# Letting GpSimd take some of the softmax scalings in a planned attention and MLP kernel

## The chip, the cores and the metric

The kernel runs on one core of a Trainium2 chip. The metric is the device time of one execution in microseconds (us); three timed runs of the kernel before gave a median of 614.84 us (614.14 to 614.98). The engines are PE (TensorE), DVE (VectorE), ACT (ScalarE), POOL (GpSimd) and SP (the queue that issues the DMAs).

## What is computed

Attention with a window of 128 keys and 4 sink keys, for 2 batches, 8 heads, 768 positions and 64 values per head; its output is taken as 1536 tokens of 512 values and goes through two MLPs with 2048 hidden values, all in float32:

```python
a = np.exp(scores - max)                      # scores outside window and sinks are -1e9
a = a / (np.sum(a, axis=-1, keepdims=True) + 1e-09)
attn = np.matmul(a, v)
h = x @ w_in;  x = (h * np.clip(h + 3.0, 0.0, 6.0) / 6.0) @ w_out       # first MLP
h = x @ w2_in; out = (h * (1.0 / (1.0 + np.exp(-1.702 * h)))) @ w2_out  # second MLP
```

## The kernel before

The attention goes over 12 tiles of 128 tokens, each in two halves of four heads, called duos (`duo`, 24 in all). A duo's steps are: the scores on PE into two PSUM banks (L756); per head, on DVE, scale, mask and row minimum (L771); per head, on ACT, the exponential with its row sum in a column of `z` (L779); one `inverse` on DVE (L787 adds 1e-9, L788 takes the reciprocal of the four sums); per head, **the scaling** `pexp <- pexp * z`, a multiplication of 128x196 numbers by one number per partition; two `turn`s on PE, eight transposes of the scaled P into PSUM (L807); copies of them to SBUF (`pts`). After two duos come the values on PE (L830, L838), and their result is split into a rounded part `xyh` (ACT) and a rest `xyl` (DVE, L857).

The MLPs multiply in three products of rounded parts and rests. A block of 512 tokens and one of 16 slices of the hidden layer make an item: the up product (L541, 12 matmuls), the activation on ACT and DVE (L553 and L558 in the first MLP), the split of its result into `gh` and `gl` (L584), and the down product (L609, 12 matmuls). Each weight slice is loaded into one of two `stage` buffers and brought into its final form once per MLP: one ACT instruction (L452) and four on DVE (L457, L465, L473, L480). A buffer is loaded again when L480 has read it. In every item the weights are split again (L430 or L432 the rounded part, L522 the rest, on DVE).

All of this is recorded as operations with a list of engines and costs in nanoseconds, and a planner (`Plan.issue`) fixes the order on each engine before the program is built. At each step it computes for every operation that is ready, and for each of its engines, when it could start (the engine free, its inputs finished, plus a fixed lag between engines) and takes the engine with the lowest score:

```python
for eng, cost in o.opts:
    x = max(t, at[eng])
    for d in o.deps:
        x = max(x, d.finish + self.lag(d.eng, eng))
    score = x + cost * (1 + early[eng])
```

`early` adds half of the cost on DVE (`PDVE` 0.5), 15 % on ACT (`PACT` 0.15) and nothing on POOL. On the chip each engine then works through its list in that order, and waits where an input is late. POOL has nothing in its list before this change but the set-up (constants, the identity, index grids).

Of the kernel before, what the change touches and what calls it, by code (L numbers as in the profile page):

```python
# [14 lines left out]
ALU = mybir.AluOpType  # L15
# [48 lines left out]
def tile_sink_window_attention_moe_moe2(  # L64
# [10 lines left out]
    nc = tc.nc  # L75
# [150 lines left out]
    with tc.tile_pool(name="msk", bufs=1) as mp:  # L226
# [15 lines left out]
            out=out, in0=grid, scalar1=x, scalar2=LOW, op0=op, op1=ALU.mult  # L242
# [185 lines left out]
    def copy(eng, out, in_):  # L428
        if eng is nc.scalar:
            eng.copy(out, in_)  # L430
        else:
            eng.tensor_copy(out, in_)  # L432
# [264 lines left out]
    def plan_attention(plan, pool, due):  # L697
# [28 lines left out]
        def duo(d, pts):  # L726

            T, half = divmod(d, 2)
            i = tok[T][1]
            kind = min(i, 2)  # L730
            front = T - 1 if i else T
            when = None
            sc = [Buf(cls="bank", kind="s") for j in range(2)]
            nbs, z = [Buf(cls="nb") for _ in range(4)], Buf(cls="z")
            pes = [Buf(cls="pexp") for _ in range(4)]

            def scores(e):

                for a in range(2):
                    hp = 2 * half + a  # L740
                    k0, q0 = hp * KW, NPAIR * KW + hp * P
                    here, before = kqt[T], kqt[front]
                    for x in range(3):
                        for c in range(2):
                            if x == 0:
                                src, at, n = before, k0, HALF
                            elif x == 1:
                                src, at, n = here, k0 + TAIL, HALF
                            elif c == 0:
                                src, at, n = before, k0 + HALF, TAIL  # L750
                            else:
                                src, at, n = here, k0, TAIL
                            for j in range(2):
                                r = slice(j * D, (j + 1) * D)
                                o = a * W + x * HALF
                                e.matmul(  # L756
                                    sc[j].tile[c * HALF : (c + 1) * HALF, o : o + n],
                                    here[r, q0 + c * HALF : q0 + (c + 1) * HALF], src[r, at : at + n],
                                    start=True, stop=True,
                                )  # L760

            plan.op(
                [("PE", 1050)], scores, when, reads=[kq_b[t] for t in sorted({front, T})], writes=sc, chain="scores",
            )
            heads = [(a, j) for a in range(2) for j in range(2)]
            for a, j in heads:
                n = 2 * a + j
                cols = slice(a * W, (a + 1) * W)
                plan.op(
                    [("DVE", 283)],  # L770
                    lambda e, j=j, n=n, cols=cols: e.tensor_tensor_reduce(  # L771
                        out=pes[n].tile[:, :W], in0=sc[j].tile[:, cols], in1=masks[kind],
                        scale=-SCALE, scalar=LOWEST, op0=ALU.add, op1=ALU.min, accum_out=nbs[n].tile,
                    ),
                    when, reads=[sc[j], mask_b[kind]], writes=[pes[n], nbs[n]],
                )
                plan.op(
                    [("ACT", 410)],
                    lambda e, n=n: e.activation(  # L779
                        pes[n].tile[:, :W], pes[n].tile[:, :W], AF.Exp,  # L780
                        bias=nbs[n].tile, scale=-1.0, accum_out=z.tile[:, n : n + 1],
                    ),
                    when, reads=[nbs[n]], writes=[pes[n]], adds=[z], chain="exp",
                )

            def inverse(e):
                e.tensor_scalar(out=z.tile, in0=z.tile, scalar1=1e-9, scalar2=None, op0=ALU.add)  # L787
                e.reciprocal(z.tile, z.tile)  # L788

            plan.op([("DVE", 280)], inverse, when, writes=[z])  # L790
            for n in range(4):

                def scale(e, n=n):
                    x, r = pes[n].tile[:, :W], z.tile[:, n : n + 1]
                    if e is nc.scalar:
                        e.mul(x, x, r)
                    else:
                        e.tensor_scalar_mul(x, x, r)

                plan.op([("DVE", 232), ("ACT", 350)], scale, when, reads=[z], writes=[pes[n]])  # L800
            for a in range(2):
                pt, pb = Buf(cls="bank", kind="t"), Buf(cls="pts")

                def turn(e, a=a, pt=pt):
                    for n in range(4):
                        j, x = divmod(n, 2)
                        e.transpose(  # L807
                            pt.tile[:, n * P : (n + 1) * P], pes[2 * a + j].tile[:, x * P : (x + 1) * P], ident
                        )

                plan.op([("PE", 440)], turn, when, reads=pes[2 * a : 2 * a + 2], writes=[pt], chain="turn")
                plan.op(
                    [("ACT", 478), ("DVE", 602)],
                    lambda e, pt=pt, pb=pb: copy(e, pb.tile, pt.tile.rearrange("p (n t) -> p n t", t=P)),
                    when, reads=[pt], writes=[pb],
                )
                pts.append(pb)
# [47 lines left out]
        for T in range(NTILE):  # L865
            pts = []
            for half in range(2):
                duo(2 * T + half, pts)
            tile_values(T, pts)

            if T + 2 < NTILE:
                load(T + 2)
# [211 lines left out]
```

## Time and profile before

| | |
|---|---|
| median of three runs | 614.84 us |
| the profiled execution, its own time | 615.07 us |
| span of the profiled execution (first to last instruction) | 613.3 us |
| busy: PE / DVE / ACT / POOL | 586.0 / 451.3 / 360.8 / 1.4 us |
| scalings of 128x196: on DVE / on ACT | 59 / 37 |

The profiled execution took 1.8 us more than its span. A busy PE is not a PE at full pace: matmuls overlap, and in a stretch where nothing is late 94 or 95 matmuls of 128x512 fit in 20 us. Idle time counts only where the engine is the one that the others wait for, so the tables by stretch say more than the totals: the attention and the first MLP's weights share the first 216 us, after that only MLP work is left.

### The profile page before, as it was taken

The page shows a single profiled execution, that of the slowest core. Times are in us where ns is not written, and L with a number is a line of the kernel's source. Part 1 is how long each engine was busy: PE and PEld are TensorE (multiplying, and loading weights), DVE is VectorE, ACT ScalarE, POOL GpSimd, SP SyncE. Part 2 cuts the span into 40 slices and gives each one's busy share as a digit, 9 for nine tenths or more (in the row PEclk, how much of TensorE's full clock was granted, in tenths as well). Part 3 has the DMA queues.
Part 4 walks back from the last instruction along what each step waited for, and adds up shares of the span by engine and source line. Part 5 has one row for each costly group of instructions (what it writes and reads, how often), then busy time and mean ns, then how long its engine had stood idle before and what let it go on. Part 6 is the DMA issues. An engine that isn't in the chain of part 4 may idle for free.

```text
span 613.3 us, 10624 instructions
## 1 busy us (share of the span) xinstructions
PE 586.0 (96%) x4242; PEld 500.3 (82%) x4242; DVE 451.3 (74%) x896; ACT 360.8 (59%) x718; POOL 1.4 (0%) x10
## 2 busy tenths in 40 slices
PE   6889999999999999999999999999999999999995
PEld 6778777787878888888878877888888888888884
DVE  7799999999995665499999999945455455455541
ACT  5897776865765764475666575544644444544442
POOL 0000000000000000000000000000000000000000
PEclk9899999999999999999999999999999999999998
DMA  8974344244430000003444334000100000200002
GB/s 265 373 231 150 131 137 155 97 160 166 131 134 1 1 2 2 0 1 137 138 137 138 137 113 161 3 0 1 51 18 0 2 1 1 69 0 1 0 1 73
DMA packets 11175, 50.91 MB, mean 83 GB/s; under 512 B 1456, under 2 KB 1456, under 8 KB 7024
## 3 DMA queue, kind: packets, MB, share of 16 engines
q1 hardware_dynamic: 11120, 50.18, 24.6%
q8 instruction: 35, 0.57, 0.4%
q14 instruction: 20, 0.16, 0.1%
HBM read 47.02 MB, written 3.15 MB: 82 GB/s over the span
## 4 chain that ended last, share of the span: by engine, by line
PE 53%; DVE 30%; ACT 6%; DMA 6%; issue 5%; POOL 0%; SPq 0%; DVEq 0%; ACTq 0%; POOLq 0%
PE bank L609 24%; PE bank L541 24%; DMA stage<-in_w_dram 5%; DVE wf L480 5%; DVE wf L473 4%; DVE w1l L522 3%; DVE w0l L522 3%; DVE gl L584 3%; DVE u L558 3%; DVE wf L457 2%; ACT pexp L779 2%; ACT wf L452 2%; DVE wf L465 2%; DVE pexp L771 2%; PE bank L756 1%
## 5 line engine op out<-in xcount | busy, mean ns | idle before, releaser
L541 PE MATMUL bank<-xyh,w0h 128*128 128x512 f32 x384 | 147.1, 383 | 0.5 <-ACT xyh L430 0.5
L541 PE MATMUL bank<-xyl,w0h 128*128 128x512 f32 x384 | 145.7, 379 | 1.0 <-DVE xyl L857 1.0
L541 PE MATMUL bank<-xyh,w0l 128*128 128x512 f32 x384 | 145.7, 379 | 0.2 <-DVE w0l L522 0.2
L522 DVE TENSOR_TENSOR w1l<-wf,w1h 128x512 fp32r<-128x512 f32 x96 | 66.0, 687 | 56.9 <-ACT w1h L430 56.9
L430 ACT CAST w1h<-wf 128x512 fp32r<-128x512 f32 x90 | 55.6, 618 | 58.5 <-PE bank L609 57.7
L430 ACT CAST gh<-u 128x512 fp32r<-128x512 f32 x91 | 56.3, 619 | 44.4 <-DVE u L558 24.8
L541 PEld LDWEIGHTS bank<-xyl,w0h 128*128 128x128 f32 x384 | 72.6, 189 | 11.1 <-DVE xyl L857 1.3
L541 PEld LDWEIGHTS bank<-xyh,w0h 128*128 128x128 f32 x384 | 72.6, 189 | 10.9 <-issue 0.6
L541 PEld LDWEIGHTS bank<-xyh,w0l 128*128 128x128 f32 x384 | 72.6, 189 | 10.8 <-DVE w0l L522 0.6
L609 PE MATMUL bank<-gl,w1h 128*128 128x512 f32 x192 | 74.4, 388 | 4.0 <-DVE gl L584 3.7
L609 PE MATMUL bank<-w1h,gl 128*128 128x512 f32 x192 | 73.4, 382 | 2.0 <-DVE gl L584 1.9
L609 PE MATMUL bank<-gh,w1h 128*128 128x512 f32 x192 | 75.0, 391 | 0.2
L609 PE MATMUL bank<-w1h,gh 128*128 128x512 f32 x192 | 72.9, 380 | 0.0
L609 PE MATMUL bank<-w1l,gh 128*128 128x512 f32 x192 | 72.8, 379 | 0.0
L609 PE MATMUL bank<-gh,w1l 128*128 128x512 f32 x192 | 72.8, 379 | 0.0
L584 DVE TENSOR_TENSOR gl<-u,gh 128x512 fp32r<-128x512 f32 x96 | 66.2, 689 | 7.0 <-ACT gh L430 2.7
L572 DVE TENSOR_TENSOR u<-bank,u 128x512 f32<-128x512 f32 x48 | 32.9, 685 | 47.5 <-ACT u L567 47.5
L522 DVE TENSOR_TENSOR w0l<-wf,w0h 128x512 fp32r<-128x512 f32 x96 | 65.5, 682 | 1.7 <-ACT w0h L430 1.5
L567 ACT ACTIVATE u<-bank 128x512 f32<-128x512 f32 x48 | 28.7, 598 | 57.1 <-PE bank L541 57.1
L452 ACT ACTIVATE wf<-stage 128x1024 f32<-128x1024 f32 x32 | 47.1, 1472 | 20.2 <-DMA stage<-in_w_dram 19.2
L430 ACT CAST w0h<-wf 128x512 fp32r<-128x512 f32 x84 | 51.4, 612 | 0.7 <-DVE wf L480 0.4
L553 ACT ACTIVATE u<-bank,three 128x512 f32<-128x512 f32 x48 | 32.8, 684 | 31.7 <-PE bank L541 31.6
(93 smaller groups left out, 817.4 us busy)
## 6 DMA issues: line engine op xcount, KB each, us to landing
stage<-in_w_dram SPq DMA_DIRECT2D x32, 1024.0 KB, 5.0
wf<-in_kq_dram SPq DMA_DIRECT2D x8, 520.0 KB, 11.1
vc<-in_vc_dram SPq DMA_DIRECT2D x12, 320.0 KB, 6.6
out_dram<-u SPq DMA_DIRECT2D x12, 256.0 KB, 2.9
vb<-in_v_dram SPq DMA_DIRECT2D x10, 256.0 KB, 6.6
kq<-in_kq_dram SPq DMA_DIRECT2D x4, 520.0 KB, 10.8
vb<-in_v_dram SPq DMA_DIRECT2D x4, 128.0 KB, 6.4
par_i<-in_params_dram SPq DMA_DIRECT2D x1, 2.0 KB, 3.0
```

Source lines behind the costliest of these rows:

```text
L430: eng.copy(out, in_)
L452: lambda e: e.activation(w.tile.bitcast(F32), top.bitcast(F32), AF.Abs),
L473: lambda e: e.scalar_tensor_tensor(out=w.tile, in0=top, scalar=-0x40000000, in1=w.tile, op0=ALU.bitwise_and, op1=ALU.bitwise_or),
L480: lambda e: e.scalar_tensor_tensor(out=w.tile, in0=low, scalar=29, in1=w.tile, op0=ALU.logical_shift_right, op1=ALU.bitwise_or),
L522: lambda e: e.tensor_tensor(out=lo.tile, in0=src.tile.bitcast(F32)[:, cols], in1=hi.tile.bitcast(F32), op=ALU.subtract),
L541: e.matmul(h.tile[:, :n], w, woven(x), start=(c == 0 and k == 0), stop=(c == NC - 1 and k == 2))
L553: lambda e: e.activation(u.tile[:, :n], h.tile[:, :n], AF.Relu, bias=three, scale=1.0),
L558: lambda e: e.scalar_tensor_tensor(out=u.tile[:, :n], in0=u.tile[:, :n], scalar=6.0, in1=h.tile[:, :n], op0=ALU.min, op1=ALU.mult,),
L567: lambda e: e.activation(u.tile[:, :n], h.tile[:, :n], AF.Sigmoid, scale=1.702),
L572: lambda e: e.tensor_tensor(out=u.tile[:, :n], in0=h.tile[:, :n], in1=u.tile[:, :n], op=ALU.mult),
L584: lambda e: e.tensor_tensor(out=gl.tile[:, :n], in0=u.tile[:, :n], in1=gh.tile[:, :n].bitcast(F32), op=ALU.subtract),
L609: e.matmul(yb.tile, l, woven(r), start=(begin and k == 0), stop=(end is not None and k == 2))
```

## The change

The scaling gets a third engine, POOL, with a planned cost of 480 ns and a form of its own (multiply by the number of the partition, then by 1.0):

```diff
                     if e is nc.scalar:
                         e.mul(x, x, r)
+                    elif e is nc.gpsimd:
+                        e.tensor_scalar(out=x, in0=x, scalar1=r, scalar2=1.0, op0=ALU.mult, op1=ALU.mult)
                     else:
                         e.tensor_scalar_mul(x, x, r)
 
-                plan.op([("DVE", 232), ("ACT", 350)], scale, when, reads=[z], writes=[pes[n]])
+                plan.op([("DVE", 232), ("ACT", 350), ("POOL", 480)], scale, when, reads=[z], writes=[pes[n]])
```

The lines behind it move by two (L798 becomes L800 for the DVE form, L798 is now the POOL form). The built programs show where the 96 scalings stand:

| duos | before: DVE, ACT | after: DVE, ACT, POOL |
|---|---|---|
| first 8 (ahead of the first MLP matmul) | 24, 8 | 14, 6, 12 |
| next 13 | 29, 19 | 13, 14, 25 |
| last 3 | 6, 6 | 5, 3, 4 |
| all | 59, 37 | 32, 23, 41 |

As the planner starts from other finishing times, it also writes the rest in another order. Two places show it.

On DVE, the two halves of tile 5 (duos 10 and 11), before; `z` is the tile of the sums, `wf4` a weight slice being brought into form:

```order
L787 TENSOR_SCALAR z_1105<-z_1105 128x4
L788 RECIPROCAL z_1105<-z_1105 128x4
L771 ISA pexp_221,nb_1211<-bank_1147,mask2_147 128x196
L771 ISA nb_1211 128x1
L798 TENSOR_SCALAR pexp_215<-pexp_215,z_1105 128x196
L798 TENSOR_SCALAR pexp_216<-pexp_216,z_1105 128x196
L798 TENSOR_SCALAR pexp_217<-pexp_217,z_1105 128x196
L465 TENSOR_SCALAR wf4_66<-wf4_66 128x1024
L787 TENSOR_SCALAR z_1197<-z_1197 128x4
L788 RECIPROCAL z_1197<-z_1197 128x4
```

The same two duos on DVE in the changed program:

```order
L787 TENSOR_SCALAR z_1087<-z_1087 128x4
L788 RECIPROCAL z_1087<-z_1087 128x4
L457 TENSOR_SCALAR wf4_66<-wf4_66 128x1024
L800 TENSOR_SCALAR pexp_215<-pexp_215,z_1087 128x196
L800 TENSOR_SCALAR pexp_217<-pexp_217,z_1087 128x196
L465 TENSOR_SCALAR wf4_66<-wf4_66 128x1024
L787 TENSOR_SCALAR z_1168<-z_1168 128x4
L788 RECIPROCAL z_1168<-z_1168 128x4
L473 SCALAR_TENSOR_TENSOR wf4_66<-stage0_60,wf4_66 128x1024
```

Of the six scalings that stood here (three more behind the second L788), two are left, and L473 of slice 4 follows at once.

On POOL, the scalings of those duos and of their neighbours, in the changed program (there were none):

```order
L798 TENSOR_SCALAR pexp_219<-pexp_219,z_943 128x196
L798 TENSOR_SCALAR pexp_214<-pexp_214,z_1087 128x196
L798 TENSOR_SCALAR pexp_216<-pexp_216,z_1087 128x196
L798 TENSOR_SCALAR pexp_218<-pexp_218,z_1168 128x196
L798 TENSOR_SCALAR pexp_221<-pexp_221,z_1168 128x196
L798 TENSOR_SCALAR pexp_215<-pexp_215,z_1411 128x196
```

A typical duo now has two scalings in a row on POOL; each waits for L788 on DVE, and a transpose on PE waits for it. The order of the matmuls on PE hardly moves: the last attention value matmul stands behind 534 MLP matmuls before and behind 531 now.

## Rows read from the trace of the kernel before

**Rows 1.** Page: span, then busy time, share of the span and instructions.

```profile
span 613.3 us, 10624 instructions
...
PE 586.0 (96%) x4242; PEld 500.3 (82%) x4242; DVE 451.3 (74%) x896; ACT 360.8 (59%) x718; POOL 1.4 (0%) x10
```

**Rows 2.** Busy time by stretch: start:end, length, engines, granted clock, DMA share, GB/s.

```profile
core 0: us, PE busy (x) PEld busy (x) DVE busy (x) ACT busy (x) POOL busy (x), PEclk, DMA share, GB/s
0.00:44.00 44.00, 33.89 (x804) 29.78 (x804) 34.53 (x159) 34.30 (x111) 1.42 (x10) 0.92 0.88 289
44.00:120.00 76.00, 72.77 (x805) 59.51 (x806) 73.94 (x197) 58.51 (x146) 0.00 (x0) 1.00 0.41 132
120.00:140.00 20.00, 20.00 (x140) 17.36 (x138) 19.76 (x27) 13.75 (x21) 0.00 (x0) 1.00 0.58 193
140.00:160.00 20.00, 18.62 (x173) 14.50 (x172) 19.29 (x49) 12.27 (x30) 0.00 (x0) 1.00 0.36 128
160.00:180.00 20.00, 20.00 (x220) 16.63 (x219) 19.39 (x34) 10.41 (x23) 0.00 (x0) 1.00 0.45 143
180.00:216.00 36.00, 35.70 (x342) 30.26 (x343) 22.25 (x64) 24.76 (x62) 0.00 (x0) 1.00 0.05 19
```

**Rows 3.** Waits between 44 and 180 us: who waited for whom, total, times, longest.

```profile
PEld bank L609 <- DVE gl L584: 2.8, 7, 0.5
PEld bank L756 <- DVE nb L771: 2.6, 6, 1.0
...
PE bank L807 <- ACT pts L430: 1.5, 1, 1.5
...
PE bank L807 <- ACT pexp L796: 0.6, 1, 0.6
```

**Rows 4.** DVE's instruction groups between 44 and 180 us: busy us, mean ns.

```profile
L480 DVE SCALAR_TENSOR_TENSOR wf<-stage,wf 128x1024 int32<-128x1024 int32 x14 | 20.4, 1460 | 0.1
...
L473 DVE SCALAR_TENSOR_TENSOR wf<-stage,wf 128x1024 int32<-128x1024 int32 x14 | 19.9, 1424 | 0.1
...
L522 DVE TENSOR_TENSOR w0l<-wf,w0h 128x512 fp32r<-128x512 f32 x19 | 13.0, 686 | 0.2
...
L584 DVE TENSOR_TENSOR gl<-u,gh 128x512 fp32r<-128x512 f32 x17 | 11.8, 694 | 0.0
L522 DVE TENSOR_TENSOR w1l<-wf,w1h 128x512 fp32r<-128x512 f32 x17 | 11.7, 687 | 0.4 <-ACT w1h L430 0.4
...
L457 DVE TENSOR_SCALAR wf<-wf 128x1024 f32<-128x1024 f32 x14 | 9.6, 690 | 0.3 <-ACT wf L452 0.3
L465 DVE TENSOR_SCALAR wf<-wf 128x1024 int32<-128x1024 int32 x14 | 9.5, 687 | 0.1
...
L798 DVE TENSOR_SCALAR pexp<-pexp,z 128x196 f32<-128x196 f32 x28 | 7.6, 316 | 0.0
```

**Rows 5.** Timeline of DVE and of ACT around 20.5 us: start, length, instruction.

```profile
20.54 0.78 DVE L798 TENSOR_SCALAR pexp<-pexp,z 128x196 f32<-128x196 f32 x3
21.24 0.35 DVE L771 CUSTOM_DVE_ANT_0 pexp<-bank,mask 128x196 f32<-128x196 f32 x1
...
20.76 0.44 ACT L796 ACTIVATE pexp<-pexp,z 128x196 f32<-128x196 f32 x1
21.11 0.44 ACT L779 ACTIVATE pexp<-pexp,nb 128x196 f32<-128x196 f32 x1
```

**Rows 6.** Timeline of POOL and of DVE around 1 us, the same columns.

```profile
0.96 0.24 POOL L228 IOTA grid<- 128x128 f32 x1
1.15 0.29 POOL masks.py:199 TENSOR_SCALAR_AFFINE_SELECT ident<-ident 128x128 f32<-128x128 f32 x1
1.40 0.18 POOL L230 IOTA colc<- 128x64 f32 x1
...
0.96 0.06 DVE L182 MEMSET least<- 128x1 f32 x1
```

## The prediction

> **What bounds the kernel now.** I read the page first: PE is busy 96 % of the span, DVE 74 %, POOL has ten small instructions [rows 1]. Taken alone this says that DVE doesn't matter. The table by stretch says otherwise [rows 2]. From 44 to 180 us DVE is busy 73.94 + 19.76 + 19.29 + 19.39 = 132.4 of 136 us, while PE is busy 72.77 of 76, 20.00 of 20, 18.62 of 20 and 20.00 of 20. After that DVE drops to 22.25 of 36 us and PE is full, so there nothing that DVE saves can be seen. In the stretch 44 to 180 PE waits at the products for `gl` (2.8 us) and at the scores for the row minima (2.6 us) [rows 3], both written by DVE. The list of DVE's groups shows what fills it: mostly the forming and splitting of weights; the scalings are 28 instructions and 7.6 us [rows 4]. From 0 to 44 us, ahead of the first MLP matmul, no engine is full: PE 33.89, DVE 34.53, ACT 34.30 of 44 us, with a DMA share of 0.88 [rows 2].
>
> **The price of a scaling.** A mean of 316 ns [rows 4] overlaps with the next instruction. The timeline gives the pitch: three scalings begin at 20.54 us and the next instruction begins at 21.24 us, so (21.24 - 20.54) / 3 = 0.233 us each on DVE; on ACT 21.11 - 20.76 = 0.35 us [rows 5].
>
> **What DVE gives away**, by the counts of the two built programs. First 8 duos: 24 to 14, 10 x 0.233 = 2.3 us. Next 13 duos: 29 to 13, 16 x 0.233 = 3.7 us. Last three: 6 to 5, 0.2 us. In all 27 scalings, 6.3 us. ACT gives away 14 x 0.35 = 4.9 us, but it is busy only 58.51 of 76 us and less after that [rows 2]: I cost this at nothing, since DVE covers it; it would count if DVE got free.
>
> **How much of that reaches the end.** First 8 duos: DVE is idle for 44 - 34.53 = 9.5 us there, and the DMAs are busy 0.88 of the time, so the relief lies between 0 and 2.3 us; I take 1.0, a little under half. Next 13 duos: a DVE second counts where PE has gaps, and PE has none in 120 to 140 and 160 to 180 us [rows 2]. That leaves 76 + 20 = 96 of 136 us, a share of 0.7. Last three duos: PE is busy 35.70 of 36 us, nothing.
>
> **What POOL takes.** The trace has no scaling on POOL. The nearest row that reads and writes SBUF there is the selection on 128x128, which began at 1.15 us with the next instruction at 1.40 us, a pitch of 0.25 us [rows 6]; by columns 0.25 x 196 / 128 = 0.38 us. Bounds: 0.25 us, if the width doesn't count, and 0.44 us, ACT's own duration for the same multiplication [rows 5]. I take 0.38. Then 41 x 0.38 = 15.6 us of POOL work lie beside other work on an engine that is empty; its queue has nothing else behind it.
>
> **Whether POOL's work slows DVE.** Not shown: the rows have the two side by side only in the set-up, where a DVE fill of 0.06 us beside a POOL index grid shows no delay, but it reads nothing [rows 6]. Bounds for one POOL scaling: DVE loses nothing, or it loses the whole 0.38 us whenever it is at an instruction that can collide. I take 0.04 us, a tenth of the upper bound, because the only row with both engines lies at zero; 25 x 0.04 = 1.0 us in the next 13 duos.
>
> **The wait that is added.** The transposes now wait for POOL. Two scalings in a row there take 2 x 0.38 = 0.76 us; the three on DVE took 0.70 us. What stands behind the waiting transposes on PE is MLP work, so each late microsecond there would be lost whole. Bounds per duo: earlier by the time that a scaling now stands behind long DVE instructions (up to 1.46 us, L480 [rows 4]), or later by 2 x 0.44 + 0.1 - 0.70 = 0.3 us. PE hardly waits for scalings in this stretch now, 0.6 us for one [rows 3]. I take 0. On SP a few loads of weights stand one or two places earlier among the others, because L480, which frees their buffer, does so on DVE; they are awaited by ACT, which has idle time [rows 2], so I cost them at nothing. If that cover goes, L452 and the forming behind it come late.
>
> **Sum.** -1.0 - 0.7 x (3.7 - 1.0) = -2.9 us. Against the profiled execution, 615.07 us (613.3 span and 1.8 around it), that is 612.2 us; on the median of the runs shown, which is 0.2 lower, 611.9; I say 612.0.
>
> **A rule against it.** Of DVE's busy 132.4 us, the instructions that read two SBUF tensors take 20.4 + 19.9 + 13.0 + 11.8 + 11.7 = 76.8 us (58 %), and those with one SBUF input and an SBUF output, L457, L465 and L798, another 26.7 us [rows 4]; together 78 %. The Trainium skill, "SBUF — State Buffer", section "Who interferes with whom", says that GpSimd has no ports of its own but shares a pair with VectorE, and that a VectorE instruction with two SBUF inputs, or in a two-port mode, and a GpSimd instruction that reads SBUF exclude each other, the later one standing still until the other has finished. No row of the kernel before shows this at work or absent. By that rule the sum would be that of the first rival.
>
> **Rivals.**
>
> *DVE stands still while POOL works (slower).* Each POOL scaling stops DVE for 0.78 x 0.38 = 0.30 us. In the next 13 duos 25 x 0.30 = 7.4 us against 3.7 us of relief: 3.7 us more on DVE, of which 0.7 count: +2.6 us. In the first 8 duos the price, 12 x 0.38 x about one half, eats the relief of 2.3 us. This gives 615.07 + 2.6 - 0.2 = 617.4 us. It decides from 3.7 / 25 = 0.15 us of DVE time per POOL scaling on. For it speaks that four fifths of what DVE does can collide; against it, that POOL's reads may be shorter than its instruction.
>
> *The two meet (no change).* At about 0.15 us per scaling the relief is eaten, or PE's gaps in 44 to 120 us turn out to be other waits: `pts`, 1.5 us in one wait, is ACT's [rows 3]. 614.8 us.
>
> *POOL is slow (slower).* If a scaling takes 0.6 us or more, two of them take 1.2 us against 0.70, and PE stands half a microsecond at the transposes. In half of the 24 duos this costs 12 x 0.5 = 6.0 us against 2.9 won: 617.9 us. It decides from about 0.5 us on. Against it speaks the row of the selection, 0.29 us long [rows 6].
>
> That the planner doesn't use POOL is no rival: 41 scalings stand on it.
>
> **How the numbers follow.** My forecast has a chance of 0.47, no change 0.20, DVE standing still 0.24, a slow POOL 0.09. About 0.2 % (1.2 us) is what a measurement of this kernel can tell from no change. So faster 0.47, within 0.20, slower 0.33. The low end takes every bound on the good side: -2.3 - 3.7 - 0.2 = -6.2 us on 614.84, 608.6 us. The high end, 618.5 us, takes in both slower cases with half a microsecond to a microsecond for transposes that come late. For the forecast alone I would say 608.6 to 613.6 us.
>
> **What would show it.** In the profile after: about 41 scalings on POOL with a pitch near 0.38 us; DVE's busy time down by 27 x 0.316 = 8.5 us, if its other groups keep their means (L473, L480, L522, L584); if these grow, or gaps open in DVE that end on nothing, DVE stands still while POOL works. PE's waits for `pexp` on POOL should be few. The last value matmul, which ended near 215 us, should come about 3 us earlier, and all behind it unchanged. I am wrong if PE waits at L807 for POOL by several microseconds, or if DVE is relieved and PE's gaps between 44 and 120 us stay.

## The result: slower, and the profile after

The changed kernel took 619.05 us (median of 5 runs, 616.96 to 620.79) against 614.84 us before: a ratio of 1.0067, with a 95 % interval of 1.0041 to 1.0094. Two later measurements on other runs gave 1.0035 [1.0016, 1.0053] and 1.0044 [1.0027, 1.0062]. The change makes the kernel slower by 0.35 to 0.7 %; the forecast was 612.0 us, faster. The profiled execution took 616.96 us (span 615.2 us), the shortest of its five runs, so the profile shows less of the loss than the median does. One later run of a version in experiment 10 (762 us) and one of the kernel before (1344 us) lie far above all the others and are left out of the medians.

The page of the changed kernel, span and busy times (before: [rows 1]):

```profile
span 615.2 us, 10689 instructions
...
PE 585.4 (95%) x4242; PEld 502.2 (82%) x4242; DVE 448.3 (73%) x869; ACT 355.9 (58%) x704; POOL 31.9 (5%) x51
```

The same stretches as in [rows 2], changed kernel; the last two rows are 10 us pieces around the end of the first 8 duos:

```profile
core 0: us, PE busy (x) PEld busy (x) DVE busy (x) ACT busy (x) POOL busy (x), PEclk, DMA share, GB/s
0.00:44.00 44.00, 32.89 (x726) 29.52 (x728) 32.52 (x149) 32.44 (x106) 9.82 (x22) 0.86 0.87 288
44.00:120.00 76.00, 71.16 (x879) 59.86 (x876) 73.60 (x177) 58.43 (x139) 12.68 (x16) 0.99 0.44 147
120.00:140.00 20.00, 19.93 (x137) 17.13 (x136) 19.45 (x35) 13.16 (x24) 3.39 (x4) 1.00 0.56 186
140.00:160.00 20.00, 18.86 (x172) 14.63 (x171) 19.84 (x45) 12.62 (x29) 1.15 (x2) 1.00 0.39 134
160.00:180.00 20.00, 19.89 (x179) 16.74 (x178) 17.13 (x34) 8.26 (x20) 1.10 (x3) 1.00 0.35 122
180.00:216.00 36.00, 36.00 (x390) 30.79 (x388) 21.49 (x62) 21.85 (x56) 3.81 (x6) 1.00 0.01 1
...
30.00:40.00 10.00, 7.93 (x178) 7.13 (x174) 8.15 (x30) 9.41 (x29) 1.97 (x3) 0.90 0.89 277
40.00:50.00 10.00, 8.19 (x160) 7.18 (x161) 7.97 (x30) 7.88 (x24) 2.78 (x5) 0.83 0.51 168
```

The kernel before, in the same two 10 us pieces:

```profile
30.00:40.00 10.00, 8.15 (x189) 6.95 (x190) 9.25 (x37) 9.63 (x31) 0.00 (x0) 1.00 0.88 269
40.00:50.00 10.00, 8.52 (x115) 7.33 (x112) 9.92 (x33) 8.08 (x24) 0.00 (x0) 1.00 0.54 178
```

The stretches that the prediction looked at, from 120 us on, are much as before, and DVE even has 2.3 us more idle time from 160 to 180 us. What is worse lies ahead: up to 50 us PE's instructions are behind (726 matmuls up to 44 us against 804), and from 40 to 50 us DVE has 2 us of idle time that it did not have, and the granted clock is 0.83 instead of 1.00. The first MLP matmul (L541) marks the end of that stage. In the timelines of PE it stands 5.0 us later:

```profile
42.52 0.45 PE L541 MATMUL bank<-xyh,w0h 128*128 128x512 f32 x1 [0.46 <-ACT xyh L430]
```

that is before; and in the changed kernel:

```profile
47.48 0.48 PE L541 MATMUL bank<-xyh,w0h 128*128 128x512 f32 x1
```

The scores of one more duo (48 matmuls) stand ahead of it now, which is 0.9 us of these 5.0. The last value matmul comes at 215.7 us against 214.8: from the first MLP matmul to it 168.2 us pass, against 172.3. That looks like the relief of DVE, but it isn't shown to be: in experiment 3, which has no scaling on POOL behind the first 8 duos, the same way takes only 166.9 us (50.92 to 217.83 us), so a late start by itself goes with a shorter way. The waits of PE between 0 and 220 us, changed kernel, show where (columns as in [rows 3]):

```profile
PEld bank L809 <- POOL pexp L798: 7.6, 7, 2.5
...
PE bank L809 <- POOL pexp L798: 5.5, 6, 2.3
...
PE bank L756 <- issue: 3.4, 1, 3.4
```

L809 are the transposes (L807 before). The longest of the six waits, 2.31 us, and one of 0.76 us come one behind the other at the eighth duo's transposes. The timeline there:

```profile
38.74 0.18 DVE L788 RECIPROCAL z<-z 128x4 f32<-128x4 f32 x1
38.84 1.19 DVE L473 SCALAR_TENSOR_TENSOR wf<-stage,wf 128x1024 int32<-128x1024 int32 x1
39.11 2.63 POOL L798 TENSOR_SCALAR pexp<-pexp,z 128x196 f32<-128x196 f32 x2 [1.79 <-DVE z L788]
39.23 0.82 ACT L796 ACTIVATE pexp<-pexp,z 128x196 f32<-128x196 f32 x2
39.95 0.35 DVE L771 CUSTOM_DVE_ANT_0 pexp<-bank,mask 128x196 f32<-128x196 f32 x1
...
40.23 1.22 DVE L480 SCALAR_TENSOR_TENSOR wf<-stage,wf 128x1024 int32<-128x1024 int32 x1
...
40.38 0.66 PE L809 MATMUL bank<-ident,pexp 128*128 128x128 f32 x4 [2.31 <-POOL pexp L798]
...
41.80 0.44 PE L809 MATMUL bank<-ident,pexp 128*128 128x128 f32 x2 [0.76 <-POOL pexp L798]
```

Two scalings on POOL take 2.63 us here, while ACT does its two in 0.82 us. PE gets the first one at 40.38 us, 0.35 us behind the end of L473 (38.84 + 1.19 = 40.03), and the second at 41.80, 0.35 us behind the end of L480 (40.23 + 1.22 = 41.45). Both are DVE instructions that read two SBUF tensors; DVE's own length for them is not longer than in [rows 4]. It is POOL that stands behind DVE, not DVE behind POOL. All scalings of the changed kernel (ns: shortest, median, longest), from the list of the tile `pexp`:

```profile
L798 POOL TENSOR_SCALAR pexp<-pexp,z x41: 422/510/2246, 10.6 to 210.7; 128x196 f32<-128x196 f32 x41
L800 DVE TENSOR_SCALAR pexp<-pexp,z x32: 303/366/496, 10.4 to 206.2; 128x196 f32<-128x196 f32 x32
```

And DVE's groups over the whole span:

```profile
L480 DVE SCALAR_TENSOR_TENSOR wf<-stage,wf 128x1024 int32<-128x1024 int32 x32 | 46.7, 1459 | 0.1
...
L473 DVE SCALAR_TENSOR_TENSOR wf<-stage,wf 128x1024 int32<-128x1024 int32 x32 | 47.3, 1479 | 0.4
...
L800 DVE TENSOR_SCALAR pexp<-pexp,z 128x196 f32<-128x196 f32 x32 | 11.3, 393 | 0.1
```

### The profile page after: what moved, and what is told of

It reads as the page before. It is cut to its first block, busy times and chain, and to the rows that moved or that the text cites. A ratio compares the mean times of both kernels' runs of the same rounds, so it can differ in the third digit from the quotient of the medians.

```text
span 615.2 us, 10689 instructions
## 1 busy us (share of the span) xinstructions
PE 585.4 (95%) x4242; PEld 502.2 (82%) x4242; DVE 448.3 (73%) x869; ACT 355.9 (58%) x704; POOL 31.9 (5%) x51
## 2 busy tenths in 40 slices
DMA packets 11176, 50.92 MB, mean 83 GB/s; under 512 B 1456, under 2 KB 1456, under 8 KB 7024
## 4 chain that ended last, share of the span: by engine, by line
PE 58%; DVE 27%; ACT 5%; issue 5%; DMA 4%; POOL 1%; SPq 0%; DVEq 0%; ACTq 0%; POOLq 0%
PE bank L609 26%; PE bank L541 25%; DVE wf L480 4%; DVE wf L473 3%; DVE w0l L522 3%; DVE u L558 2%; DVE w1l L522 2%; DMA stage<-in_w_dram 2%; DVE wf L457 2%; DVE gl L584 2%; DVE wf L465 2%; ACT wf L452 2%; PE bank L809 2%; PE bank L756 2%; PE bank L832 2%
## 5 line engine op out<-in xcount | busy, mean ns | idle before, releaser
L541 PE MATMUL bank<-xyh,w0h 128*128 128x512 f32 x384 | 147.6, 384 | 0.6 <-ACT pts L430 0.4
L541 PE MATMUL bank<-xyh,w0l 128*128 128x512 f32 x384 | 145.5, 379 | 0.7 <-issue 0.7
L541 PE MATMUL bank<-xyl,w0h 128*128 128x512 f32 x384 | 145.5, 379 | 0.0
L430 ACT CAST w1h<-wf 128x512 fp32r<-128x512 f32 x94 | 58.1, 618 | 62.1 <-PE bank L609 61.4
L541 PEld LDWEIGHTS bank<-xyh,w0h 128*128 128x128 f32 x384 | 72.5, 189 | 12.2 <-issue 0.9
L541 PEld LDWEIGHTS bank<-xyh,w0l 128*128 128x128 f32 x384 | 72.6, 189 | 10.3
L541 PEld LDWEIGHTS bank<-xyl,w0h 128*128 128x128 f32 x384 | 72.6, 189 | 9.7
L430 ACT CAST w0h<-wf 128x512 fp32r<-128x512 f32 x81 | 49.6, 612 | 0.1
```

The lines of the kernel that those rows point to most:

```text
L541: e.matmul(h.tile[:, :n], w, woven(x), start=(c == 0 and k == 0), stop=(c == NC - 1 and k == 2))
```

## The experiments

The theory after this profile: the loss arises ahead of the first MLP matmul, where the planner's new order meets POOL scalings that are late. Rivals: DVE is slowed by POOL; the loss lies behind the first 8 duos; the new order alone is enough.

**1. New order, no scaling on POOL.** What the plan puts on POOL is executed on DVE at the same place.

```diff
-                o.fn(ENG[eng])
+                o.fn(ENG["DVE" if eng == "POOL" else eng])
```

> The changed plan with its order on every engine, but the 41 scalings that it gave to POOL are issued on DVE at their place. Theory A (POOL's scaling stands still while DVE is in an instruction with two SBUF inputs, PE waits for it at the transposes, and the PE clock falls after the idle time): PE's waits for POOL (7.6 us) go, DVE gets 41 x 0.233 = 9.6 us more work, 14 scalings more than the kernel before had: 614 to 617 us, mean granted clock at 0.990 or above. Theory B (DVE stands still while POOL works): 14 x 0.233 x 0.7 = 2.3 us above before, 617 us, and L800 back at a mean of 316 ns. Theory C (the other order of the plan costs the time, not POOL): 618 us or more, as the changed kernel.

Measured: 621.31 us, ratio 1.0095 [1.0078, 1.0112]. That is the number of the theory that the new order costs the time (618 us or more), and above what the two others expected. In this order the kernel is slower still without POOL: an order that was planned with POOL is a bad one without it. PE's long stop at the eighth duo's transposes is there too, with no scaling on POOL (PE, then DVE):

```profile
40.42 1.09 PE L809 MATMUL bank<-ident,pexp 128*128 128x128 f32 x8 [2.37 <-DVE pexp L800]
...
38.94 1.20 DVE L473 SCALAR_TENSOR_TENSOR wf<-stage,wf 128x1024 int32<-128x1024 int32 x1
...
40.05 0.55 DVE L800 TENSOR_SCALAR pexp<-pexp,z 128x196 f32<-128x196 f32 x2
```

DVE goes through L473 first and scales behind it; PE resumes 0.28 us behind the end of L473 (38.94 + 1.20 = 40.14), against 0.35 us with POOL. In the kernel before, the transposes of the seventh and eighth duo run through without a stop:

```profile
36.77 2.46 PE L807 MATMUL bank<-ident,pexp 128*128 128x128 f32 x16
```

So most of the 2.31 us belongs to the new order, whichever engine scales: in the changed kernel PE stops at 40.38 - 2.31 = 38.07 us, and L788, for which all scalings of the duo wait, ends only at 38.92 us. The first MLP matmul began at 46.5 us here.

**2. POOL only behind the first 8 duos** (28 scalings on it), twice.

```diff
-                plan.op([("DVE", 232), ("ACT", 350), ("POOL", 480)], scale, when, reads=[z], writes=[pes[n]])
+                plan.op([("DVE", 232), ("ACT", 350)] + ([("POOL", 480)] if d >= 8 else []), scale, when, reads=[z], writes=[pes[n]])
```

> POOL is offered only from the ninth duo on (28 scalings on it); the first 8 duos are planned as in the kernel before. Theory A, with the loss in the first 48 us and a small win behind: no half-speed stretch of the PE clock beyond those of before, PE waits for POOL below 3 us: 612 to 614.5 us. Theory B: DVE loses more than it gives away where it is full: 616 to 618 us. Theory C: between 615 and 619 us, by the luck of the order.

> The kernel that offers POOL only after the first 8 duos once more, beside the three others on one chip. Theory: 0.997 to 1.000 of before, as the first time (0.9989), the first MLP matmul at 42.3 to 43 us. If the first time was chance: above 1.001.

Measured: 614.86 us, ratio 0.9989 [0.9977, 1.0001], and 615.62 us, 0.9990 [0.9976, 1.0005]. The loss is gone when POOL is kept out of the first 8 duos; what is left is level with the kernel before or 0.1 % faster. It is the fastest version that leaves nothing out, and neither interval excludes no change. The first MLP matmul began at 42.6 us in the first profile, as before; in the second at 44.6 us, though the program is the same. That start scatters by some 2 us from one execution to the next, and one profile alone proves little about it.

**3. POOL only in the first 8 duos** (`if d < 8` in the same place; 12 scalings on it).

> POOL is offered only in the first 8 duos (12 scalings on it); the order of PE there is the changed kernel's, and the later duos are planned without POOL. Theory D (formed from the first four runs: the loss lies in the first 8 duos, where the new order lets PE run dry twice, ahead of scores whose instructions have not come and ahead of the last duo's transposes, and the granted clock falls to half after each; the later duos win about 2 us): first MLP matmul near 47 us, at least one extra half-speed stretch, and without the later win the slowest of all, 618 to 622 us. Theory A as first put (POOL's blocked scalings cost the time wherever they stand): 12 of 41 scalings, about 616 us.

Measured: 616.77 us, ratio 1.0013 [0.9996, 1.0030]. The profile has the late start (first MLP matmul at 50.9 us, the same wait of 2.31 us for POOL), but the time lost is less than I expected. The effects of this version and of the one before add up to 0.02 to 0.03 %, not to the 0.35 to 0.7 % of the whole: the plan behind the first 8 duos is another in each, so the two halves of the change can't simply be added.

**4. POOL fills instead of multiplying**, all 41 tiles, order unchanged. The kernel leaves out these 41 multiplications, and a fill doesn't wait for `z` either.

```diff
-                        e.tensor_scalar(out=x, in0=x, scalar1=r, scalar2=1.0, op0=ALU.mult, op1=ALU.mult)
+                        e.memset(x, 0.005)
```

> The changed plan, but POOL fills its tile with a constant instead of multiplying (this leaves out the multiplication of 41 of the 96 tiles by one over their sum), so that it reads nothing from SBUF; same order, same tiles. Theory A: POOL's instructions all last about 0.26 us, none above 0.5; PE's waits for POOL fall from 7.6 to below 1 us: 611 to 614 us. Theory B: the DVE instructions L800 and L787 come back to their means of before, 612 to 615 us. Theory C: 617 us or more.

Measured: 616.38 us, ratio 1.0009 [0.9996, 1.0022]. A fill takes 262 ns in the median and 877 at most, and PE waits for none of them. Against the changed kernel (1.0035 on the same chip, experiment 6) most of the loss is gone, but the 611 to 614 us that I expected did not come. The first MLP matmul still began at 46.6 us, 4.1 us later than before, behind a stop of 1.63 us at the eighth duo that ended on ACT, with the clock at 1.00 from 40 to 50 us. So part of the lateness comes with the order alone.

**5. The kernel before with POOL at work beside it**: 48 multiplications of a spare tile that nobody waits for, two per duo (the lines that lay out the spare tile are left out of the cut).

```diff
+                    if n < 2:
+                        nc.gpsimd.tensor_scalar(
+                            out=junk, in0=junk, scalar1=r, scalar2=1.0, op0=ALU.mult, op1=ALU.mult
+                        )
```

> The kernel before, unchanged in plan and order, and beside it 48 multiplications of a spare 128x196 tile on POOL, two per duo, by the numbers in z, whose result nobody reads. Theory A: POOL's instructions last 0.45 us where DVE is at instructions that cannot collide and up to 2 us where it is at L473 or L480; DVE's groups keep their means within 2 %, only L798 grows (to about 350 to 385 ns); 614.5 to 616 us. Theory B: L473, L480, L522 grow, DVE loses 48 x 0.15 = 7 us or more and the time is 618 us or more.

Measured: 616.64 us, ratio 1.0015 [1.0003, 1.0027], 1.0 us more than before. Its groups:

```profile
L480 DVE SCALAR_TENSOR_TENSOR wf<-stage,wf 128x1024 int32<-128x1024 int32 x32 | 47.4, 1480 | 0.2
L473 DVE SCALAR_TENSOR_TENSOR wf<-stage,wf 128x1024 int32<-128x1024 int32 x32 | 47.1, 1472 | 0.3
...
L797 POOL TENSOR_SCALAR spare<-spare,z 128x196 f32<-128x196 f32 x48 | 30.2, 630 | 173.7 <-DVE z L789 78.4 <-ACT u L553 68.8 <-ACT pexp L780 15.2
...
L803 DVE TENSOR_SCALAR pexp<-pexp,z 128x196 f32<-128x196 f32 x59 | 18.6, 363 | 0.1
```

DVE is busy for 455.2 us against 451.3, so 3.9 / 48 = 0.08 us per POOL instruction. The long two-input instructions keep their means over the whole span (1479 and 1460 before); what grows is DVE's own scaling, 363 ns against 317. POOL's takes 630 ns in the mean. DVE hardly loses, POOL does.

**6. Keeping PE at work** with 16 matmuls of the identity ahead of the eighth duo's transposes, in the changed kernel, to see whether the clock's fall is what costs; beside it the changed kernel once more.

```diff
+                    if d == 7 and a == 0:
+                        for _ in range(16):
+                            e.matmul(pt.tile[:, :P], ident, ident, start=True, stop=True)
```

> The changed kernel, and ahead of the first transposes of the eighth duo 16 more matmuls of 128x128 on PE, whose result the transposes overwrite; they fall into the 2.3 us in which PE waits there. Theory D with the clock as half of the loss: the half-speed stretch near 42 us does not come, the first MLP matmul comes 1 to 2 us earlier, 617 to 618 us, about 1.5 us below the changed kernel. If the clock is only a sign and the scalings' chain is the cause: as the changed kernel or up to 1 us above it.

> The changed kernel once more, beside the next three on the same chip: 617 to 621 us, two extra stretches of the PE clock at half speed (near 28 and 42 us), first MLP matmul near 47 us against 42.5 before.

Measured: 619.49 us, 1.0043 [1.0025, 1.0060], beside 617.90 us, 1.0035 [1.0016, 1.0053]. No gain, though the granted clock stayed at 1.00 from 40 to 50 us; its first MLP matmul began at 51.4 us, behind another stop of PE of 3.0 us for which the trace names no releaser. Inconclusive on the clock: the other stop, and what the filling itself delays, stand in the way.

**7. POOL behind the first 8 duos at a planned cost nearer to its mean** (900 instead of 480; 14 scalings on it).

> POOL is offered from the ninth duo on at a planned cost of 900 ns instead of 480, near what its scalings took behind DVE (mean 0.8 us); 14 scalings on it instead of 28. Theory A and D: PE's waits for POOL fall below 1 us, DVE still gives some scalings away: 613 to 615.5 us, at or below e2. If POOL's help comes by the number of scalings: above e2, at the kernel before.

Measured: 616.24 us, 1.0018 [0.9992, 1.0044]. A truer price halved the scalings on POOL and did not make a better plan.

**8. Old order, POOL in the first 8 duos.** The kernel before, in which 13 of DVE's 24 scalings of the first 8 duos are executed on POOL; no plan changes.

```diff
+                    elif d < 8 and n % 2 == 0:
+                        nc.gpsimd.tensor_scalar(
+                            out=x, in0=x, scalar1=r, scalar2=1.0, op0=ALU.mult, op1=ALU.mult
+                        )
```

> The kernel before with its own order on every engine, in which 13 of the 24 scalings that DVE did in the first 8 duos are executed on POOL (every second head, where the plan had put it on DVE); nothing else moves. Theory (the new order ahead of the first MLP matmul is what costs): the first MLP matmul begins at 42.3 to 43.5 us, as before, PE has no 3 us wait for its own issue near 27 us, and the time is 0.999 to 1.002 of before. Rival (executing scalings on POOL in the first 8 duos is what costs, because each takes 0.5 us and up to 2.6 us behind L473 or L480): the first MLP matmul begins at 45 us or later, PE waits for POOL at the transposes for 3 us or more in all, ratio 1.003 to 1.006.

Measured: 616.06 us, ratio 1.0002 [0.9984, 1.0019]; first MLP matmul at 41.8 us. PE waits for POOL 2.9 us in two waits, both at the first two transpose groups (2.25 us before 11.08 us, 0.61 before 12.79), where the kernel before waits 2.20 and 0.81 us for DVE; so POOL adds no wait here. POOL's work in the first 8 duos is not in itself what costs; it costs in the order that the planner writes for it.

**9. The version of 2 with fills, and with DVE, in place of POOL's 28 multiplications** (the edits of 4 and 1).

> The kernel that offers POOL only after the first 8 duos, in which POOL fills its 28 tiles with a constant instead of multiplying (28 of the 96 multiplications are left out); order unchanged. If what POOL's reading and its standing behind DVE costs there is small (PE waited 2.0 us for POOL there in the run before): 0.5 to 1.5 us faster than that kernel on the same chip, ratio to before 0.997 to 0.9985. If POOL's execution costs nothing there: level with it within 0.5 us.

> The kernel that offers POOL only after the first 8 duos, with its order, but the 28 scalings that the plan puts on POOL are executed on DVE at the same places. If the relief of DVE behind the first 8 duos is worth 0.7 of its DVE time: 28 x 0.233 x 0.7 = 4.6 us slower than that kernel on the same chip, ratio to before 1.004 to 1.007. If DVE's relief reaches no end there: level with it, 0.998 to 1.000.

Measured beside the second run of 2 (615.62 us): with fills 614.16 us, 0.9976 [0.9962, 0.9990]; with DVE 616.79 us, 1.0012 [0.9999, 1.0026]. There, POOL instead of DVE is worth 616.79 - 615.62 = 1.2 us, not the 4.6 us of a full 0.7 per microsecond of DVE; fills, which are shorter and wait for no `z`, are worth 616.79 - 614.16 = 2.6 us.

**10. The changed kernel, cut at the first 8 duos.** Four kernels with the changed order on one chip: fills in the first 8 duos only (12 of the 41), fills behind them only (29), the changed kernel itself, and the 29 executed on DVE.

```diff
+                    elif e is nc.gpsimd and d < 8:
+                        e.memset(x, 0.005)
```

(`d >= 8` for the second; `nc.vector.tensor_scalar_mul(x, x, r)` with `d >= 8` for the fourth.)

> The changed kernel with its order; POOL's 12 tiles of the first 8 duos are filled with a constant (these 12 multiplications are left out), the 29 behind are multiplied on POOL. If POOL's price lies at duo 8's transposes (3.07 us of waits for POOL there in the changed kernel): no wait of PE for POOL before the first MLP matmul, and 1 to 3 us faster than the changed kernel beside it, ratio to before about 1.001. If the order alone makes the first MLP matmul late: that matmul still begins at 45 us or later and the time is within 1 us of the changed kernel.

> The changed kernel with its order; the 12 tiles of the first 8 duos are multiplied on POOL, the 29 behind are filled with a constant (29 multiplications left out). If POOL's price lies ahead of the first MLP matmul: only the 1.5 us that the same edit saved in the kernel that offers POOL after the first 8 duos (616.25 of 615.62 less 614.16), and still 1.001 to 1.003 of before. If the larger part of POOL's price lies behind: 2 us or more faster than the changed kernel beside it.

(The difference meant in the brackets is 615.62 less 614.16.)

> The changed kernel itself, as the measure for the three others on the same chip. 1.0035 to 1.0067 of before, as the two times before; the first MLP matmul at 46 us or later.

> The changed kernel with its order; the 12 scalings of the first 8 duos run on POOL, the 29 behind that the plan puts on POOL are executed on DVE at the same places. If POOL is worth as much behind the first 8 duos as in the kernel that offers it only there (1.2 us): 1 to 1.5 us slower than the changed kernel beside it. If the two parts of the change disturb each other (the sum of their two measured effects, 1.0013 and 0.999, is less than the 1.0035 of the whole): level with it or faster.

Measured against 616.33 us before:

| changed order, POOL's share in | first 8 duos | behind | us | ratio |
|---|---|---|---|---|
| the changed kernel | multiplies | multiplies | 618.32 | 1.0044 [1.0027, 1.0062] |
| | fills | multiplies | 616.51 | 1.0003 [0.9984, 1.0022] |
| | multiplies | fills | 618.79 | 1.0046 [1.0029, 1.0062] |
| | multiplies | on DVE | 621.67 | 1.0103 [1.0077, 1.0128] |

Twelve multiplications in the first 8 duos go with nearly the whole loss: without them, the same order is level with the kernel before (by the medians 1.8 us of the 2.0 us are gone; by the means 2.4 us, 95 % interval 1.1 to 3.6). That is against fills, which have no multiplication to do. Against DVE, POOL shows no extra cost there: with all 41 on DVE (experiment 1) the ratio is 1.0095, with only the 29 on DVE it is 1.0103. The 29 behind cost nothing against fills, where I had expected 1.5 us, and on POOL they are worth 621.67 - 618.32 = 3.35 us against DVE in the same order, more than the 1 to 1.5 us expected. The kernel with fills in the first 8 duos, at the place shown above; its profiled execution is the fastest of its twelve, 613.62 us against a median of 616.51:

```profile
37.98 1.20 DVE L473 SCALAR_TENSOR_TENSOR wf<-stage,wf 128x1024 int32<-128x1024 int32 x1
...
39.25 0.88 PE L811 MATMUL bank<-ident,pexp 128*128 128x128 f32 x6 [1.71 <-ACT pexp L796]
...
44.34 0.48 PE L541 MATMUL bank<-xyh,w0h 128*128 128x512 f32 x1 [0.68 <-ACT xyh L430]
```

and the changed kernel beside it:

```profile
40.23 1.19 DVE L473 SCALAR_TENSOR_TENSOR wf<-stage,wf 128x1024 int32<-128x1024 int32 x1
40.50 2.63 POOL L798 TENSOR_SCALAR pexp<-pexp,z 128x196 f32<-128x196 f32 x2 [1.79 <-DVE z L788]
...
41.77 1.11 PE L809 MATMUL bank<-ident,pexp 128*128 128x128 f32 x4 [2.31 <-POOL pexp L798]
...
43.19 0.69 PE L809 MATMUL bank<-ident,pexp 128*128 128x128 f32 x2 [0.31 <-POOL pexp L798]
...
49.75 0.48 PE L541 MATMUL bank<-xyh,w0h 128*128 128x512 f32 x1
```

PE's stop is 1.71 us instead of 2.31 + 0.31, and it goes through six matmuls at once. The 1.71 us end on ACT's scalings, which wait for the same `z`. Of the 5.4 us between the two first MLP matmuls, 1.9 us were there before the stop (PE stood from 37.54 us in the one and from 39.46 us in the other). From its resumption to the first MLP matmul pass 44.34 - 39.25 = 5.1 us in the one and 49.75 - 41.77 = 8.0 us in the other. The kernel with fills behind the first 8 duos, whose PE stood from 37.50 us, resumed at 39.82 and began the first MLP matmul at 47.79 us, again 8.0 us later. The 48 value matmuls and their weight loads in between, which wait for nothing, show the clock: from 40.05 to 42.02 us with fills, and from 44.23 to 47.84 us in the changed kernel, 1.6 us longer:

```profile
40.05 0.44 PE L834 MATMUL bank<-pts,vb 128*64 128x128 f32 x4
...
42.02 0.34 PE L756 MATMUL bank<-wf,wf 64*64 64x64 f32 x8
```

```profile
44.23 0.70 PE L832 MATMUL bank<-pts,vb 128*64 128x128 f32 x4
...
47.84 0.49 PE L756 MATMUL bank<-wf,wf 64*64 64x64 f32 x8
```

The stretch from 40 to 50 us with fills:

```profile
40.00:50.00 10.00, 9.07 (x172) 7.93 (x171) 9.10 (x30) 9.24 (x25) 1.59 (x3) 1.00 0.59 173
```

and in the changed kernel beside it:

```profile
40.00:50.00 10.00, 7.93 (x153) 7.01 (x154) 7.95 (x29) 8.02 (x24) 3.54 (x4) 0.66 0.54 170
```

At 0.66 about 6.8 of these 10 us were granted 1.2 GHz instead of 2.4. It is no chance of one execution: worked out from the mean granted clock of each run, (1 - clock) x 2 x time, the changed kernel spent 18.6 us at the lower level in the median of its 12 runs, the one with fills 12.9 us, the kernel before 12.3 us. But the version of experiment 3 spent 19.1 us there and lost only 0.9 us, so time at the lower level is not the loss itself.

## Why the prediction was wrong

**The step that failed is "The wait that is added", taken as 0.** I compared two scalings in a row on POOL (0.76 us) with three on DVE (0.70 us), and looked for PE's waits in the stretch from 44 to 180 us [rows 3]. The wait that costs lies ahead of that stretch, at the eighth duo's transposes near 40 us, where the two scalings took 2.63 us and PE stood 3.07 us. Most of the first stop is there without POOL too, 2.37 us with the scalings on DVE (experiment 1) and 1.71 us with fills. I had priced the step, and of the new order only SP's loads; that L788 and L473 now stand later than PE needs them was not in the sum. The scaling itself I had priced by a row from the set-up [rows 6], in which DVE has no long instruction beside POOL; there was none of the kind to read, and my upper bound, 0.44 us, took no account of what DVE does at the same time. Measured were 0.42 us at least, 0.51 in the median, 0.75 in the mean and 2.25 at most.

**"First 8 duos ... I take 1.0"** was wrong in sign for the same reason. A stage in which no engine is full [rows 2] behaves here like a chain, in which the length of a step counts, not an engine's load. The planner put L473 right behind L788 on DVE, which is the instruction that releases POOL; so POOL began 0.27 us behind L473 and stood behind it, then behind L480. The reorder was costed at nothing. With fills the kernel is level with the one before; with POOL's multiplications ahead of the first MLP matmul it takes 1.8 us more, by the medians of experiment 10. That the eighth duo's place carries this is read from the profiles and was not tested by itself.

**Next 13 duos:** "a share of 0.7" gave -1.9 us. That DVE's work counts in this stage held: in the same order, 29 scalings on POOL instead of DVE are worth 3.35 us (experiment 10), 0.5 per microsecond of the 29 x 0.233 = 6.8 us, and 28 are worth 1.2 us (experiment 9), 0.2 of 6.5 us. In the version that offers POOL only there, the time fell by 615.65 - 614.86 = 0.8 us and 616.24 - 615.62 = 0.6 us, about a third of the forecast, with no change inside both intervals. Multiplying instead of filling costs 1.5 us there (experiment 9), which the changed kernel's order does not show again (experiment 10); so this price hangs on the order, and I have no single number for it.

**"POOL's work slows DVE by 0.04 us":** 0.08 us (experiment 5), well below the 0.15 us from which the first rival decides. Even so, DVE's busy time fell by 3.0 us only, not 8.5: its scalings take 15.8 - 11.3 = 4.5 us less (393 ns each instead of 317), and small growth elsewhere eats the rest.

**The rivals.** *DVE stands still while POOL works* is refuted in the direction that it names: L473 and L480 keep their length, and POOL stands still; only DVE's own scalings grow, from 317 to 363 and 393 ns. The Trainium skill, "SBUF — State Buffer", section "Who interferes with whom", which I cited for it, says that the one that comes later stands still; the trace agrees with that, 2.63 us for two scalings that take 0.84 to 1.17 us in nine of the twelve other pairs, and what I missed is that DVE, which is hardly ever idle, is nearly always the earlier one. The same section says that an instruction which only writes SBUF does not meet a two-input one; the fills of experiment 4 agree, 0.26 us beside L473 at 26.91 us. The longest there, 0.88 us at 38.77 us, began with L465, which has one SBUF input. *POOL is slow* came nearest: it named PE's stop at the transposes, a decision from about 0.5 us and 617.9 us. But it spread half a microsecond over 12 duos, where one duo has 3.07 of the 5.5 us, and most of that duo's stop does not need a slow POOL (experiment 1). I had given it 0.09.

**What would show it** was right as a test: "wrong if PE waits at L807 for POOL by several microseconds". It does.

**Open.** How the 1.8 us divide between PE's longer stop and the lower clock behind it: the value matmuls took 1.6 us longer at the lower clock in the profile, but experiment 6 did not show that this reaches the end. Why the late start costs 0.9 us with POOL in the first 8 duos alone but more in the whole change. And what stops PE for 1.8 to 3.4 us near 27 us, in the middle of the scores and on no semaphore, in the kernels with the changed order; here in the changed kernel:

```profile
27.32 0.27 PE L756 MATMUL bank<-wf 64*64 64x64 f32 x1 [3.43 <-issue]
```

The DMAs are fully busy then (a share of 1.02 from 20 to 30 us). The kernel before has a stop of this kind too, of 2.1 us at 25.5 us. The kernel with fills in the first 8 duos has this stop too (3.42 us) and is level with the kernel before, so it is not the main cause; its own cause was not tried.

## What to carry to other kernels

Before an idle engine is given part of a chain, price its step beside what the neighbour engine does at that very moment, and not from a quiet stretch: here the same instruction took 0.42 to 2.25 us. A planner with one fixed cost per operation can't see that, and a new option rewrites the whole order: read the new order for where an input now comes later than the engine at the end of the chain needs it, as L788 and L473 did here. Offer the extra engine only where the relieved engine is the bound: kept to the duos behind the first 8, the same change cost nothing and by the medians gained 0.1 %, which neither interval tells from no change.

## What the runs showed of the hardware

- A POOL multiplication of 128x196 numbers takes 0.42 us at least and 0.51 in the median, and up to 2.25 us (2.82 in experiment 10's run of the changed kernel) beside DVE instructions with two SBUF inputs, which lose nothing themselves (means of 1460 to 1480 ns with and without it).
- A DVE scaling beside POOL's work takes 363 to 393 ns in the mean instead of 317, although it reads one SBUF tensor and one number per partition.
- In six profiles with POOL's multiplications at the eighth duo and nothing to fill the wait, PE's stop of 2.3 us goes with a granted clock of 0.66 to 0.83 from 40 to 50 us and a first MLP matmul 5.0 to 8.4 us later than before; with DVE's scalings there (2.37 us) the clock was 0.83 and the matmul 4.0 us late. In the two profiles with fills, in the same order, the stops were 1.63 and 1.71 us, the clock stayed at 1.00, and the matmul came 4.1 and 1.8 us late.
